# u's row moved to ScalarE's DMA queue, and its product moved behind the turning of the first k, in an RWKV and channel-mixing kernel

## The chip, the core and the metric

The kernel runs on one core of a Trainium2 chip. The metric is device microseconds of one execution: the median over several runs, and beside it one execution taken with the hardware profiler, from which all rows below come. TensorE does the matrix products, VectorE, ScalarE and GpSimd the element-wise work, and SyncE and ScalarE issue the transfers from HBM, each on a queue of its own.

## What is computed

The inputs r, k and v have shape (4, 8, 768, 48): batch, heads, steps, width of a head. Each head carries a 48x48 state that decays by w and takes in k times v; u weighs the present step's own pair. The result, laid out as (4, 768, 384), goes through a low-rank mixing over the steps (U, V) and a two-layer MLP.

```python
for t in range(S):
    cur = np.einsum('bhd,bhe->bhde', u[None] * kt, vt)
    y[:, :, t] = np.einsum('bhd,bhde->bhe', rt, state + cur)
    state = w[None, :, :, None] * state + np.einsum('bhd,bhe->bhde', kt, vt)
...
xt = x.transpose(0, 2, 1)
h = xt @ U @ V
u = x + h.transpose(0, 2, 1)
ch = np.maximum(u @ w_ch1, 0.0) @ w_ch2
return (u + ch)
```

## The kernel before

Each batch's 768 steps are cut into six chunks of 128. For a chunk n the recurrence becomes products of matrices:

- r and k are turned (transposed on TensorE against an identity, four products each, `a_tr`, L831; tiles ptr and ptk) and scaled with powers of w (rT and kT; L840 to L854).
- The score products of rT and kT (L1017) write two banks, bank_tr and bank_sc. VectorE masks them into am (L1025). TensorE multiplies am by v into pav (L1066), adds what the state of the chunks before gives (SW by rT, L1072), and collects the next state in psu (L1039).
- ks is k times a table of powers (L782). dv is the step's own term: r times k, times ub (both on GpSimd, L791), summed over a head on VectorE (dg, L798), times v (L804 on VectorE, L802 on ScalarE). VectorE adds pav and dv into x (L1085).

ub holds u on all 128 partitions. `load_ub` (L471 to L476) makes it: a DMA of 1x384 values into urow, one product p_u of a column of ones by urow, which copies the row to all partitions, and a copy to ub on ScalarE.

After the six chunks of the first batch comes what the prediction calls the G stage: x times U is gathered (c_gx, L1185, into the bank wake; gf and Gs, L1198 to L1220), V is split into parts (v_parts, L666; pv, V), x is turned (pu), and the columns uTh and uTl (high and low halves, L1268 and L1269) go into the MLP. Its first layer is p<-uTh,w1s and p<-uTl,w1s; hh and hl (L1479, L1480) are the high and low half of its result, and w2s holds the second layer's weights. The weights are unpacked and split on VectorE, ScalarE and GpSimd (L608 to L655). The MLP of one batch overlaps the recurrence of the next and runs from about 40 us to the end.

No instruction stands in its final place in the code. Every step is an operation with a key, an estimated duration, the buffers that it reads and writes, and one or more engines that can do it. `Plan.schedule` (L180 ff.) walks through time with its own estimates and picks on each engine the ready operation of the smallest key; an added `dk` shifts one operation's key. Each engine then works through its list strictly in that order. `follow` adds a semaphore wait: an element-wise operation on GpSimd waits for a VectorE operation planned just ahead, since the two engines share a port. TensorE's gaps in the plan are filled with dummy products (`wake<-still`), whose results nobody reads.

The steps that the change touches get their keys here:

```python
at(-101, lambda: ends.append(pe(214, fill, [wk], [])))
...
at(-100, lambda: load_pairs(w, wq))
at(-99, lambda: a_load(0))
...
at(UB, load_ub)
```

`a_load(n)` issues the three loads of chunk n; k of the first three chunks goes through ScalarE's queue, r and v through SyncE's. The keys of turning chunk 0's k and r are 5.0 and 5.2.

Of the kernel before, what the change touches and what calls it, by code (L numbers as in the profile page):

```python
# [47 lines left out]
class Plan:  # L48
# [36 lines left out]
    def op(self, eng, ns, fn, w=(), r=(), alt=(), lock=False, dma=0.0, rows=0, late=0.0, tiled=False, dk=0.0):  # L85


        if self.direct:
            fn()
            return None  # L90
        o = Op()
        o.n = len(self.ops)
        o.key = (self.key + dk, o.n)
        o.ways = [(eng, ns, fn, lock)] + list(alt)
        o.dma, o.rows, o.late, o.tiled = dma, rows, late, tiled
        o.deps, o.behind, o.allocs, o.bufs = set(), set(), [], []
        for acc, write in [(a, False) for a in r] + [(a, True) for a in w]:
            b, sub = acc if isinstance(acc, tuple) else (acc, None)
            if not b.uses and b.tag:
                o.allocs.append(b)  # L100
                ring = self.rings.setdefault(b.tag, {"order": [], "next": 0, "free": [(-99.0, "")] * b.bufs, "last": None})
                ring["order"].append(b)
            elif b.tag and b.uses[0][0] is not o:
                o.behind.add(b.uses[0][0])
            for p, s, pw in b.uses:
                if (write or pw) and (s is None or sub is None or s == sub) and p is not o:
                    o.deps.add(p)
            b.uses.append((o, sub, write))
            if b not in o.bufs:
                o.bufs.append(b)  # L110
                b.left += 1
        self.ops.append(o)
        return o
# [207 lines left out]
def rwkv_moe(ctx: ExitStack, tc: tile.TileContext, r, k, v, w, u, U, V, w1, w2, out):  # L321
# [9 lines left out]
    DM = H * D  # L331
# [28 lines left out]
    def wbuf(shape, dt, tag, bufs, name):  # L360
        return Buf(work, shape, dt, tag, bufs, name)
# [6 lines left out]
    def bank(tag, name):  # L368
        made = Buf(ps, [128, 512], F32, tag, {"mm": 2, "acc": 3}.get(tag, 1), name)
        if tag in ("tr", "sc"):  # L370
            if tag not in lasting:
                lasting[tag] = ps.tile([128, 512], F32, name=f"bank_{tag}", tag=tag, bufs=1)
            made.got = lasting[tag]
        return made

    def f32(ap):
        return ap.bitcast(F32)
# [4 lines left out]
    def whole(*args, **kw):  # L382

        opened.clear()
        return nc.tensor.matmul(*args, **kw)  # L385

    def pe(ns, fn, w_, r_, tiled=False, dk=0.0):
        return op("PE", ns, fn, w_, r_, tiled=tiled, dk=dk)

    def on_dve(n, fn, w_, r_, port=False, dk=0.0):  # L390
        return op("DVE", dve(n), lambda: fn(nc.vector), w_, r_, lock=port, dk=dk)

    def on_act(n, fn, w_, r_, times=1, dk=0.0):
        return op("ACT", times * (act(n) - 94) + 94, fn, w_, r_, dk=dk)
# [10 lines left out]
    def dma(fn, w_, r_, rows, run, eng="SP", ns=470, dk=0.0, late=0.0, either=False):  # L405

        q = nc.scalar if eng == "ACT" else nc.sync
        return op(eng, ns, lambda: fn(q), w_, r_, dma=rows * max(1.05, run / 320),
                  rows=rows, late=late, dk=dk, alt=[("ACT", ns, lambda: fn(nc.scalar), False)] if either else ())
# [5 lines left out]
    one_ = const.tile([1, 1], F32, name="one")  # L415
# [54 lines left out]

    def load_ub():  # L471
        urow = wbuf([1, DM], F32, "xh", NXS, "urow")
        dma(lambda q: q.dma_start(urow.t, u.rearrange("(o h) d -> o (h d)", o=1)), [urow], [], 1, 1536, ns=500)
        pt = bank("av", "p_u")
        pe(650, lambda: whole(pt.t[:, :DM], lhsT=one_.broadcast_to([1, 128]), rhs=urow.t, start=True, stop=True), [pt], [urow])
        on_act(384, lambda: nc.scalar.copy(ub.t, pt.t[:, :DM]), [ub], [pt])  # L476

    def table(i):
# [1182 lines left out]
    def at(t, f):  # L1661
        steps.append((t, len(steps), f))
# [5 lines left out]
    NEXT_W1, SOON = (18, 20), 16.0  # L1668
    MORE = {}
    FRONT, EACH = 9.0, 4.5  # L1670
    UB = -98.5
    VR, DVK, DV = 35.97, 1, -1.0
    LATE_DG = 4
    PWI, KD = 0.0, False
# [13 lines left out]
    for i, n_ in ((0, 2), (5, 1)):  # L1688
        at(-50, lambda i=i, n_=n_: on_dve(128 * n_, lambda e: e.memset(f32(sel.t[:, :, i:i + n_]), 0.0), [(sel, i)], []))
    at(UB, load_ub)  # L1690
    backs = []
    at(-97, lambda: backs.append(powers()))
# [144 lines left out]
```

## Time and profile before

| | us |
|---|---|
| median of 3 runs | 398.85 (398.24 to 399.52) |
| profiled execution | 398.65 |
| its span, first to last instruction | 396.9 |
| TensorE busy | 388.8 (98%) |
| VectorE, ScalarE, GpSimd busy | 302.3, 140.5, 97.9 |
| mean granted TensorE clock | 0.996 |

The span is the profiled execution without what lies before the first and after the last instruction (1.75 us). Busy time counts instructions of the engine itself, and a product's end is modelled, so 98% says that TensorE has nearly always an instruction in flight, not that it runs at its peak.

### The profile page before, as it was taken

The numbers are of one execution on the slowest core, as the hardware profiler recorded it, in microseconds if no ns is written. First come the engines' busy times: TensorE is split into PE (matmuls) and PEld (weight loads), VectorE is DVE, ScalarE is ACT, GpSimd is POOL, SyncE is SP. The second block draws the span as 40 slices with busy tenths as digits, with TensorE's granted clock in tenths as the row PEclk, the third lists the DMA queues.
The fourth block names the chain that finished last, engine by engine and source line by source line (L and its number), as shares of the span: only waits on it lengthen the run. The fifth ranks groups of instructions, "written<-read, shape, count | busy, mean of one in ns | idle before, by whom it ended". The sixth has DMA issues, their size and how long they took to land.

```text
span 396.9 us, 11718 instructions
## 1 busy us (share of the span) xinstructions
PE 388.8 (98%) x4808; PEld 374.3 (94%) x4808; DVE 302.3 (76%) x685; ACT 140.5 (35%) x355; POOL 97.9 (25%) x150
## 2 busy tenths in 40 slices
PE   7999999999999999999999999999999999999994
PEld 6897999999999999999999999999999999999994
DVE  6999999999999849887794588999444874455453
ACT  3378757646541422101012242541132422232210
POOL 2882142532434024331010132354000200100000
PEclk9999999999999999999999999999999999999998
DMA  9988899698759686864797768600136110000003
GB/s 147 180 212 220 166 225 255 101 201 219 132 93 208 103 192 104 150 96 86 126 157 112 142 166 130 119 2 3 61 58 143 40 61 0 2 1 2 0 3 124
DMA packets 189852, 45.08 MB, mean 114 GB/s; under 512 B 174686, under 2 KB 188256, under 8 KB 189792
## 3 DMA queue, kind: packets, MB, share of 16 engines
q1 hardware_dynamic: 186240, 43.08, 55.9%
q10 hardware_dynamic: 3552, 1.18, 1.3%
q8 instruction: 40, 0.66, 0.7%
q14 instruction: 20, 0.16, 0.2%
HBM read 36.57 MB, written 7.67 MB: 111 GB/s over the span
## 4 chain that ended last, share of the span: by engine, by line
PE 96%; DMA 1%; SPq 0%; ACT 0%; DVE 0%; issue 0%
PE p L385 65%; PE c L385 9%; PE pav L914 3%; PE pav L920 3%; PE bank_sc L385 2%; PE bank_tr L385 2%; PE bank_tr L1017 2%; DMA urow<-in_u_dram 1%; PE pav L1066 1%; PE bank_tr L894 1%; PE bank_tr L880 1%; PE bank_tr L1185 1%; PE pav L1072 1%; PE ptr L831 1%; PE pu L385 1%; PE psu L1039 1%
## 5 line engine op out<-in xcount | busy, mean ns | idle before, releaser
L385 PE MATMUL p<-uTh,w1s 128*128 128x384 f32 x432 | 111.5, 338 | 0.0
L385 PE MATMUL p<-w2s,hh 128*128 128x384 f32 x528 | 111.2, 339 | 0.0
L385 PEld LDWEIGHTS p<-w2s,hh 128*128 128x128 f32 x528 | 92.2, 188 | 1.4 <-ACT hh L1479 0.2
L1479 ACT ACTIVATE hh<-p 128x384 fp32r<-128x384 f32 x72 | 35.4, 491 | 136.2 <-PE p L385 123.9
L385 PEld LDWEIGHTS p<-uTh,w1s 128*128 128x128 f32 x432 | 77.1, 188 | 0.6
L385 PE MATMUL p<-uTl,w1s 128*128 128x384 f32 x216 | 72.4, 335 | 0.0
L385 PE MATMUL p<-w2s,hl 128*128 128x384 f32 x264 | 62.4, 335 | 0.0
L1480 DVE SCALAR_TENSOR_TENSOR hl<-p,hh 128x384 fp32r<-128x384 f32 x72 | 39.8, 553 | 28.9 <-ACT hh L1479 28.0
L385 PEld LDWEIGHTS p<-w2s,hl 128*128 128x128 f32 x264 | 47.2, 188 | 0.2 <-DVE hl L1480 0.2
L385 PEld LDWEIGHTS p<-uTl,w1s 128*128 128x128 f32 x216 | 40.5, 188 | 0.0
L781 POOL MEMSET ks<- 128x128 f32 x24 | 4.8, 206 | 70.9 <-PE bank_tr L894 70.9
L914 PEld LDWEIGHTS pav<-vsw,am 64*64 64x64 f32 x288 | 17.4, 134 | 4.5 <-issue 3.3
L1406 ACT ACTIVATE hh<-v 128x384 fp32r<-128x384 f32 x18 | 9.3, 526 | 34.8 <-DVE v L1397 31.9
L914 PE MATMUL pav<-vsw,am 64*64 64x48 f32 x288 | 19.8, 221 | 0.0
L1397 DVE TENSOR_TENSOR v<-c,s 128x384 f32<-128x384 f32 x18 | 9.9, 555 | 12.6 <-PE c L385 12.5
L914 PE MATMUL pav<-ldv,am 64*64 64x48 f32 x288 | 19.3, 221 | 0.0
L920 PE MATMUL pav<-S,rT 48*64 48x48 f32 x528 | 19.1, 218 | 0.0
L1317 POOL TENSOR_TENSOR uTl<-ut,uTh 128x384 fp32r<-128x384 f32 x4 | 4.1, 1015 | 59.1 <-ACT uTh L1316 59.1
L385 PE MATMUL c<-uTh,w1s 128*128 128x384 f32 x72 | 18.5, 338 | 0.0
L920 PEld LDWEIGHTS pav<-S,rT 48*64 48x64 f32 x528 | 17.3, 135 | 0.0
L791 POOL TENSOR_TENSOR dv<-dv,ub 128x384 f32<-128x384 f32 x12 | 12.1, 1012 | 20.3 <-DVE w2s L655 8.9
L914 PEld LDWEIGHTS pav<-ldv,am 64*64 64x64 f32 x288 | 16.9, 134 | 0.0
(253 smaller groups left out, 782.8 us busy)
## 6 DMA issues: line engine op xcount, KB each, us to landing
raw_w<-in_moe_w_ch_dram SPq DMA_DIRECT2D x24, 384.0 KB, 4.9
out_dram<-x SPq DMA_DIRECT2D x21, 192.0 KB, 2.7
ldr<-in_r_dram SPq DMA_DIRECT2D x20, 192.0 KB, 3.8
ldk<-in_k_dram SPq DMA_DIRECT2D x20, 192.0 KB, 4.2
ldv<-in_v_dram SPq DMA_DIRECT2D x20, 192.0 KB, 4.2
bl<-in_r_dram SPq DMA_DIRECT2D x79, 48.0 KB, 2.9
bl<-in_k_dram SPq DMA_DIRECT2D x79, 48.0 KB, 2.5
ub<-ud SPq DMA_DIRECT2D x15, 192.0 KB, 2.8
```

The costliest lines, as they stand in the source:

```text
L385: return nc.tensor.matmul(*args, **kw)
L781: op("POOL", 250, lambda: nc.gpsimd.memset(ks.t[:, :, D:], 0.0), [(ks, "pad")], [])
L791: on_either(384, lambda e, a_=a_, b_=b_: e.tensor_mul(dv.t, a_()[:, :, :D], b_()[:, :, :D]), w_, r_, only="POOL" if front(n) else None)
L831: nc.tensor.transpose(pt.t[:PD, q * C:(q + 1) * C], src().rearrange("p h d -> p (h d)")[:, q * PE_:q * PE_ + PD], ident_)
L914: return nc.tensor.matmul(to(q, j, i), lhsT=am[j].t[half, q, :], rhs=vsw[n].t[half, q, :] if j else vt()[half, 2 * q, :], start=((alone or ...
L920: return nc.tensor.matmul(to(q, row, i), lhsT=rT.t[rows, q, i * C2:(i + 1) * C2], rhs=St[n, i].t[rows, q, :], start=False, stop=((alone or ...
L1017: return nc.tensor.matmul(abs_[n][j].t[:, q * C:(q + 1) * C], lhsT=kT.t[rows, q, :], rhs=rT.t[rows, q, :], start=True, stop=True)
L1317: on_either(384, lambda e: e.tensor_tensor(ul.t[:, ct, :], ut.t, f32(uh.t[:, ct, :]), ALU.subtract), [(ul, ct)], [ut, (uh, ct)])
L1397: on_dve(384, lambda e: e.tensor_tensor(to.t, pt.t[:, :TB], other.t, ALU.add), [to], [pt, other])
L1406: on_act(384, lambda: nc.scalar.activation(hh.t, value(), AF.Relu), [hh], [src])
L1479: on_act(384, lambda: nc.scalar.activation(hh.t, pt.t[:, :TB], AF.Relu), [hh], [pt])
L1480: on_dve(384, lambda e: e.scalar_tensor_tensor(hl.t, pt.t[:, :TB], 0.0, f32(hh.t), ALU.max, ALU.subtract), [hl], [pt, hh])
```

## The change

urow's DMA is issued by ScalarE instead of SyncE. p_u gets a key of its own: -98.9 + 104 = 5.1, between the turning of chunk 0's k (5.0) and of its r (5.2), where it was -98.5. `UB` itself moves from -98.5 to -98.9, so the load comes right behind the loads of chunk 0 either way.

```diff
     def load_ub():
         urow = wbuf([1, DM], F32, "xh", NXS, "urow")
-        dma(lambda q: q.dma_start(urow.t, u.rearrange("(o h) d -> o (h d)", o=1)), [urow], [], 1, 1536, ns=500)
+        dma(lambda q: q.dma_start(urow.t, u.rearrange("(o h) d -> o (h d)", o=1)), [urow], [], 1, 1536, ns=500, eng="ACT")
         pt = bank("av", "p_u")
-        pe(650, lambda: whole(pt.t[:, :DM], lhsT=one_.broadcast_to([1, 128]), rhs=urow.t, start=True, stop=True), [pt], [urow])
+        pe(650, lambda: whole(pt.t[:, :DM], lhsT=one_.broadcast_to([1, 128]), rhs=urow.t, start=True, stop=True), [pt], [urow], dk=104.0)
...
-    UB = -98.5
+    UB = -98.9
```

Since the plan is made anew, other instructions move too. TensorE's list at the start, in which ld_97 and ld_116 are the loads of chunks 0 and 1, was:

```order
3 L831 MATMUL ptk_132<-ident,ld_97 112x128 x4
4 L385 MATMUL wake<-still 128x128 x2
5 L831 MATMUL ptr_148<-ident,ld_97 112x128 x4
6 L500 MATMUL pt_tabf<-ident,back 128x112 x4
7 L385 MATMUL wake<-still 128x128 x3
8 L385 MATMUL p_u<-urow,one 128x384
9 L1017 MATMUL bank_tr<-rT_170,kT_155 128x128
...
17 L831 MATMUL ptr_200<-ident,ld_116 112x128 x4
18 L831 MATMUL ptk_208<-ident,ks_113 112x128 x4
```

And it is now the following, where ld_121 is the load of chunk 1:

```order
3 L831 MATMUL ptk_133<-ident,ld_97 112x128 x4
4 L385 MATMUL p_u<-urow,one 128x384
5 L831 MATMUL ptr_149<-ident,ld_97 112x128 x4
6 L500 MATMUL pt_tabf<-ident,back 128x112 x4
7 L385 MATMUL wake<-still 128x128 x3
8 L831 MATMUL ptr_182<-ident,ld_121 112x128 x2
9 L1017 MATMUL bank_tr<-rT_173,kT_156 128x128
...
17 L831 MATMUL ptr_182<-ident,ld_121 112x128 x2
18 L831 MATMUL ptk_204<-ident,ks_111 112x128 x4
```

p_u stands in the place of the two dummy products ahead of the first r, and two of the four products that turn chunk 1's r have moved from behind the eight score products to the place ahead of them.

GpSimd's list for chunks 1 to 3, with the semaphores that each instruction waits for, was (dv_227 and dv_304 are the dv tiles of chunks 1 and 2, ks_256 the ks of chunk 2):

```order
26 L782 TENSOR_TENSOR ks_256<-ld_122,tabf 128x8x48 [waits DMAHW4_49]
27 L791 TENSOR_TENSOR dv_227<-dv_227,ub 128x384 [waits DVE_49,Pool_49]
28 L791 TENSOR_TENSOR dv_304<-ld_122 128x384 [waits DMAHW1_49]
29 L735 MEMSET ldr_317 128x8x16
30 L781 MEMSET ks_325 128x8x16 [waits PE_49]
31 L782 TENSOR_TENSOR ks_325<-ld_184,tabf 128x8x48 [waits DMAHW4_49]
```

The same place now, with chunk 1's dv called dv_236 and chunk 2's dv_306:

```order
26 L782 TENSOR_TENSOR ks_268<-ld_126,tabf 128x8x48 [waits DMAHW6_49,DVE_49,Activation_49]
27 L791 TENSOR_TENSOR dv_236<-dv_236,ub 128x384 [waits Pool_49]
28 L791 TENSOR_TENSOR dv_306<-ld_126 128x384 [waits DMAHW1_49]
29 L735 MEMSET ldr_319 128x8x16
30 L781 MEMSET ks_333 128x8x16 [waits PE_49]
31 L782 TENSOR_TENSOR ks_333<-ld_195,tabf 128x8x48 [waits DMAHW4_49,DVE_49]
```

The second dv product of chunk 1 no longer waits for VectorE; the ks products do instead.

VectorE's list at the G stage was (x_768 is the x of chunk 5):

```order
72 L1085 TENSOR_TENSOR x_768<-pav_0_707,dv_594 128x4x48
73 L1085 TENSOR_TENSOR x_768<-pav_1_733,dv_594 128x4x48
74 L655 TENSOR_TENSOR w1s_765<-raw_w_0_469,w1s_765 128x384
75 L655 TENSOR_TENSOR w1s_770<-raw_w_1_489,w1s_770 128x384
76 L615 SCALAR_TENSOR_TENSOR raw_w_0_472<-raw_w_0_472 128x384
77 L615 SCALAR_TENSOR_TENSOR raw_w_2_625<-raw_w_2_625 128x384
78 L1220 TENSOR_TENSOR Gs_787<-wake,Gs_787 32x384
```

It is now, with chunk 5's x called x_760:

```order
73 L1085 TENSOR_TENSOR x_760<-pav_0_708,dv_583 128x4x48
74 L1085 TENSOR_TENSOR x_760<-pav_1_720,dv_583 128x4x48
75 L615 SCALAR_TENSOR_TENSOR raw_w_0_477<-raw_w_0_477 128x384
76 L608 TENSOR_SCALAR raw_w_2_633<-raw_w_2_633 128x384
77 L618 SCALAR_TENSOR_TENSOR raw_w_0_477<-raw_w_0_477 128x384
78 L655 TENSOR_TENSOR w1s_777<-raw_w_0_470,w1s_777 128x384
79 L655 TENSOR_TENSOR w1s_783<-raw_w_1_488,w1s_783 128x384
80 L655 TENSOR_TENSOR w2s_788<-raw_w_0_477,w2s_788 128x384
81 L1220 TENSOR_TENSOR Gs_796<-wake,Gs_796 32x384
```

Six instructions instead of four stand between the last x and Gs. On TensorE, the pv products of that stage, which stood between the two halves of chunk 5's pav and behind gf, now stand ahead of both.

## Rows read from the trace of the kernel before

**Rows 1.** The page: busy time by engine, and the chain by line.
```profile
PE 388.8 (98%) x4808; PEld 374.3 (94%) x4808; DVE 302.3 (76%) x685; ACT 140.5 (35%) x355; POOL 97.9 (25%) x150
...
PE p L385 65%; PE c L385 9%; PE pav L914 3%; PE pav L920 3%; PE bank_sc L385 2%; PE bank_tr L385 2%; PE bank_tr L1017 2%; DMA urow<-in_u_dram 1%; PE pav L1066 1%; PE bank_tr L894 1%; PE bank_tr L880 1%; PE bank_tr L1185 1%; PE pav L1072 1%; PE ptr L831 1%; PE pu L385 1%; PE psu L1039 1%
```

**Rows 2.** The chain in order of time, 0 to 13: start us, us, what.
```profile
2.82 5.75 DMA urow<-in_u_dram
...
8.62 0.91 PE p_u L385 x2
```

**Rows 3.** Timeline of PE: start us, us, instruction [idle before <-releaser].
```profile
4.06 1.02 PE L831 MATMUL ptk<-ident,ld 128*112 128x128 f32 x4
...
6.62 0.66 PE L831 MATMUL ptr<-ident,ld 128*112 128x128 f32 x4 [1.09 <-DMA ld<-in_r_dram]
...
7.49 0.85 PE L385 MATMUL wake<-still 128*128 128x128 f32 x6
...
9.46 0.37 PE L1017 MATMUL bank_tr<-rT,kT 48*128 48x128 f32 x1
...
10.55 0.65 PE L831 MATMUL ptr<-ident,ld 128*112 128x128 f32 x4
11.03 0.60 PE L831 MATMUL ptk<-ident,ks 128*112 128x128 f32 x4
...
16.26 0.43 PE L831 MATMUL ptr<-ident,ld 128*112 128x128 f32 x2
16.62 0.67 PE L1066 MATMUL pav<-ld,am 128*64 128x48 f32 x16
```

**Rows 4.** Timeline of SyncE's queue: DMA issues.
```profile
2.82 0.92 SPq L473 DMA_DIRECT2D urow<-in_u_dram  x1
3.79 0.53 SPq L731 DMA_DIRECT2D ld<-in_r_dram  x1
```

**Rows 5.** Timeline of DVE.
```profile
7.55 1.12 DVE L844 SCALAR_TENSOR_TENSOR rT<-ptr,wif,pw 112x128 f32<-112x128 f32 x4
...
10.65 0.69 DVE L1025 TENSOR_TENSOR am<-bank_tr,before 128x512 f32<-128x512 f32 x1 [1.05 <-PE bank_sc L1017]
...
13.18 1.22 DVE L804 TENSOR_TENSOR dv<-ld,dg 128x384 f32<-128x384 f32 x1
14.32 0.68 DVE L1025 TENSOR_TENSOR am<-bank_tr,before 128x512 f32<-128x512 f32 x1
...
27.14 0.55 DVE L804 TENSOR_TENSOR dv<-ldv,dg 128x384 f32<-128x384 f32 x1
```

**Rows 6.** DMA issues in 3.5 to 4.2 us: KB each, us from issue to landing.
```profile
ld<-in_r_dram SPq DMA_DIRECT2D x1, 192.0 KB, 6.3
```

**Rows 7.** Windows: each engine's busy us, then granted clock, DMA share, GB/s.
```profile
8.00:9.00 1.00, 0.72 (x5) 0.44 (x4) 1.00 (x4) 0.17 (x1) 0.00 (x0) 1.00 1.47 164
...
391.00:392.00 1.00, 0.66 (x4) 0.34 (x2) 0.30 (x1) 0.00 (x0) 0.00 (x0) 1.00 0.46 169
...
393.00:394.00 1.00, 0.00 (x0) 0.00 (x0) 0.00 (x0) 0.00 (x0) 0.00 (x0) 0.99 0.88 309
```

**Rows 8.** Timeline of POOL.
```profile
12.99 0.99 POOL L782 TENSOR_TENSOR ks<-ld,tabf 128x384 f32<-128x384 f32 x1
14.54 1.01 POOL L791 TENSOR_TENSOR dv<-dv,ub 128x384 f32<-128x384 f32 x1 [0.56 <-DVE dv L804]
```

**Rows 9.** Timeline at the G stage: PE and DVE.
```profile
33.59 0.52 PE L385 MATMUL pv<-v_parts,sel 128*96 128x192 f32 x4 [0.50 <-ACT gf L1198]
...
40.14 0.51 PE L385 MATMUL p<-uTh,w1s 128*128 128x384 f32 x2
...
37.96 0.55 DVE L1220 TENSOR_TENSOR Gs<-wake,Gs 32x384 fp32r<-32x384 f32 x1
```

**Rows 10.** Timeline in the MLP: DVE's hl and PE's use of it.
```profile
85.85 0.56 DVE L1480 SCALAR_TENSOR_TENSOR hl<-p,hh 128x384 fp32r<-128x384 f32 x1
...
89.00 0.68 PE L385 MATMUL p<-w2s,hl 128*128 128x384 f32 x3
```

## The prediction

> **What bounds the kernel now.** I read the page first, then the chain, then the timeline of the first 45 us engine by engine, and the windows last. TensorE is busy for 388.8 of 396.9 us, and 96% of the chain is its own work; the only other piece of size is the transfer of u's row, 1% [rows 1]. The chain shows where: 5.75 us from the issue of that row, then the product p_u, 0.91 us, then chunk 0's score products [rows 2]. So the time is TensorE's work plus what it waits or fills with dummy products at the start, and something gained or lost there reaches the end only if it survives the stages between. The timeline of TensorE shows the gaps: 1.09 us before it can turn the first r, three dummy products from 7.49 to 8.34 (x6: each counts twice in the trace), p_u, and the scores at 9.46 [rows 3]. What the change takes away is the wait for urow, and p_u's place between the dummies and the scores.
>
> **The change, part by part.** *The row and its product.* urow goes out on ScalarE's queue right behind the first k, so at about 1.3 us instead of 2.82, with one 192 KB transfer ahead of it in that queue; on SyncE's it had two [rows 4]. TensorE turned that k at 4.06, so it had landed by then [rows 3], and I estimate the row at 4 to 5 us. p_u then runs behind the turning of k, in the stretch before 6.62 in which TensorE has two dummy products and waits 1.09 us [rows 3], and its 0.91 us are covered. If they are not (a row later than 5.7), they push the turn of r, and VectorE's four rT pieces at 7.55 follow that turn by 0.3 us at the earliest; the cost is then at most 0.9. With p_u gone from 8.6, the scores wait only for the rT pieces, which end at 8.67 [rows 5], and could start at about 8.7 instead of 9.46: a gain of up to 0.75 us. That is what the edit offers.
>
> *What stands in its way.* The kernel's planner lays out everything anew, and the order shows half of the second r's turning (two of four products) now ahead of chunk 0's scores. TensorE works in order, so the scores now wait for the second r to land. Before, that r was issued at 3.79 [rows 4] and took 6.3 us [rows 6]: it landed at 10.09. Without urow in SyncE's queue its issue moves up by 0.97 (3.79 less 2.82). Does the landing move too? The DMA engines were saturated when it travelled (a share of 1.47 and 164 GB/s between 8 and 9 us [rows 7]), the queue ahead of it holds the same two transfers, and the second and third k, which now go out behind urow, take bandwidth late instead of early. So it can gain nothing (10.09) or the whole 0.97 (9.12); I take 10.09, since bytes and not the issue are what it waited for.
>
> The Trainium skill's page "Trainium Kernel Development and Optimization", section "Key Constraints", says that transfers from all queues run on the same 16 DMA engines and interleave, and that issuing from several engines saves the sequencer's issue time alone. By that rule the landing stays near 10.09 and the scores are late; by the queue alone it would be 9.12. Row 8:9 of the windows agrees with the rule.
>
> *Front, summed.* Half a turn takes 0.36 us of TensorE (16.26 to 16.62, the half that before had split off in chunk 1 [rows 3]), so the scores start at 10.09 + 0.36 = 10.45, 0.99 later than 9.46. Behind the scores only the other half is left of a whole turn's 0.48 (10.55 to 11.03), so 0.24 comes back. TensorE is +0.75 at the second k's turning.
>
> *The shared port.* VectorE hangs on the scores: its mask products, 10.65 before [rows 5], start at 11.64; rT, dg and S follow, and its product dv (L804), 13.18 before, is ready at 14.17. GpSimd does not wait for it any more: before, its second dv product of chunk 1 stood at 14.54 because it waited 0.56 us for L804 [rows 8]; the order now shows it waiting for GpSimd's own work alone. It follows ks (12.99 before, whose memset waits for TensorE's psu, +0.1 to +0.2) and starts at about 14.05. What two such instructions do to each other shows in L804 itself: 1.22 us beside GpSimd's product of 12.99 to 13.98, 0.55 alone at 27.14 [rows 5, 8]. So L804 now waits from 14.17 to 15.06 and ends at 15.6; both x (0.27 each, as half as wide) and the mask product follow, at 16.1 instead of 14.32 (the order now puts both x ahead of it). Part of this +1.8 is eaten: both x stood between the two mask products before, so the second of these is only +1.2; the half turn that stood between pav and pav is gone (0.36); and the scores of chunk 2 start some +0.75 late. The whole turn behind them costs 0.24 more than the half of before. I carry +0.95 through chunks 2 to 5, which run at TensorE's own pace.
>
> *The G stage.* Chunk 5's part changes order as well. The pv products waited 0.50 us for ScalarE's gf [rows 9]; now they stand ahead of pav and wait for v_parts alone: +0.95 - 0.50 = +0.45 when the last x is made. But gf and ScalarE's Gs now come behind four casts, and VectorE's Gs, 37.96 before, behind six instructions instead of four since the last x, the two more at 0.35 to 0.55 each (L804's 0.55 alone is one of that width [rows 5]): +0.45 + 0.9 = +1.35 at Gs [rows 9], of which dummy products and turnings that are independent of it take up some 0.35 behind it. The first MLP product, 40.14 before [rows 9], comes at about +1.0. All six pu products are then done, of which two stood behind the first MLP units before; at 0.17 each (the pitch of a 384-column product) that gives 0.34 back: **+0.65**. With the r at 9.5 or earlier the same sum keeps +0.35, since the G stage costs about that by itself.
>
> *The MLP.* From there on the chain is TensorE's own [rows 1], and the order has the same 2858 instructions on it, so a shift at the entrance passes through to the end. VectorE takes 1.3 to 3.6 us more work ahead of the low halves hl (the count of added rows times their durations), and an hl stands ready some 2.6 us before its use (85.85 + 0.56 to 89.00 [rows 10]); other gaps are up to 7. I price this at nothing; its bound is the surplus over the smallest gap, 1 us, twice over in a long stage.
>
> **Rivals.** *Lost port (slower).* A waiting VectorE might lose the port a second time: GpSimd has the next product, dv of chunk 2, standing right behind, at 15.0. Then L804 starts at 16.0, and each of chunks 1 to 3 that repeats it adds about 1 us: +3.2, some 402. Nothing in the trace of before shows VectorE waiting across two back-to-back GpSimd products, so arbitration is open; it decides if L804 takes over 2 us.
> The Trainium skill's page "SBUF — State Buffer", section "Who interferes with whom", says that the order of issue decides who blocks and that the other blocks fully. By it L804 loses once, as in the sum; 1.22 against 0.55 agrees.
> *MLP stalls (slower).* The added VectorE work does overrun the slack, or TensorE's 1.75 us of nothing before 10.09 (dummies end at 8.34) takes its clock down: +1.3 to +2.3, 400.0 to 401.6. Against the clock: it was busy for 0.66 of the microsecond from 391 and then no more, and the granted clock was still 0.99 from 393 to 394 [rows 7], after over a microsecond without work; before, the longest gap at the start was 1.09 [rows 3]. Against the stalls: 2.6 us of slack.
> *The gain arrives (faster).* The second r lands at 9.1 or before, L804 misses the contention because everything comes earlier, and the G stage keeps its 0.50: -0.7 to -1.5, 397.2 to 398.0. For it: a one-transfer shorter queue and p_u's 0.75. Against it: saturated engines, and Gs behind more work.
>
> **How the numbers follow.** The sum stands against the profiled execution of 398.65, 0.20 below the median of three runs: 399.3 by the one and 399.5 by the median, so 399.4. A change under 0.3%, 1.2 us, is about what a measurement of this kernel cannot tell from none. Chances: the sum or anything within 1.2 of before, 0.55; lost port 0.10 and MLP stalls or clock 0.17, together 0.27 slower; the gain 0.18. The range leaves out the far end of the lost port and of the gain: 397.5 to 401.2.
>
> **What would show it.** Right: urow landed before 5.5 and p_u before the turn of r; TensorE idle before the half turn with the second r as releaser, 1.5 us or more; scores at 10.4; L804 of chunk 0 at about 1.4 us from when it was ready; no pv wait for gf; first MLP product at 40.8 to 41.3. Wrong: scores before 9.5, L804 at 0.55, waits of PE behind hl after 40 us, or a granted clock under 1 before 30 us.

## The result, and the profile of the changed kernel

The change makes the kernel slower by 0.5%: a median of 401.37 us over 22 runs against 399.12 us over 22 runs of the kernel before, a ratio of 1.0052 (95% interval 1.0034 to 1.0070). One execution of the changed kernel, at 428 us, was disturbed and is left out of the ratio and of the counts below. The profiled execution of the changed kernel took 400.71 us with a span of 398.9 us, 2.0 more than the span of before; of this, 1.78 us stand at the last matrix product (393.11 against 391.33) and the rest in the last transfers behind it.

The page and the chain first. TensorE is busy for 2.6 us longer than in [rows 1], and the transfer of u's row is gone from the chain; in its place the chain has 1% of VectorE. TensorE's list is no longer than before (x4805 in the page against x4808), so it is busier because it waits less (1.9 us in all up to 45 us, against 2.9) and because some products ran slower: p_u alone takes 1.64 us where it took 0.91 [rows 2]. The last section comes back to this.

```profile
PE 391.4 (98%) x4805; PEld 375.3 (94%) x4805; DVE 303.1 (76%) x691; ACT 142.7 (36%) x372; POOL 91.2 (23%) x144
...
PE 94%; DVE 1%; POOL 0%; ACT 0%; issue 0%; ACTq 0%
```

The timeline of TensorE at the start answers to [rows 3]:

```profile
4.04 1.10 PE L831 MATMUL ptk<-ident,ld 128*112 128x128 f32 x4
5.08 1.64 PE L385 MATMUL p_u<-urow,one 1*128 1x384 f32 x2
6.65 1.10 PE L831 MATMUL ptr<-ident,ld 128*112 128x128 f32 x4
...
8.29 1.51 PE L385 MATMUL wake<-still 128*128 128x128 f32 x6
10.19 0.41 PE L831 MATMUL ptr<-ident,ld 128*112 128x128 f32 x2 [0.39 <-DVE ks L782]
10.53 0.37 PE L1017 MATMUL bank_tr<-rT,kT 48*128 48x128 f32 x1
...
15.99 0.65 PE L831 MATMUL ptk<-ident,ks 128*112 128x128 f32 x4 [0.30 <-POOL ks L782]
```

p_u runs behind the turning of k without a wait, and r is turned right behind it, at 6.65 against 6.62. Then comes the half turn of chunk 1's r, at 10.19, and the scores of chunk 0 start 1.07 us later than before. The releaser printed there is VectorE's ks, which ended at 10.08; the r of chunk 1 landed at 10.02, so the two came almost together, and e7 below shows the r alone. The issue of that r on SyncE's queue moved from 3.79 [rows 4] to 2.82, and the transfer took 7.2 us instead of 6.3 [rows 6]:

```profile
2.82 1.48 SPq L731 DMA_DIRECT2D ld<-in_r_dram  x1
```

```profile
ld<-in_r_dram SPq DMA_DIRECT2D x1, 192.0 KB, 7.2
```

GpSimd and VectorE, which answer to [rows 8] and [rows 5]: here L804 takes 0.55 us, alone, and it is GpSimd that waits, with the ks of chunk 2 behind the L804 of chunk 0.

```profile
14.93 1.00 POOL L782 TENSOR_TENSOR ks<-ld,tabf 128x384 f32<-128x384 f32 x1 [1.44 <-ACT SW L1055]
15.89 1.00 POOL L791 TENSOR_TENSOR dv<-dv,ub 128x384 f32<-128x384 f32 x1
```

```profile
14.25 0.55 DVE L804 TENSOR_TENSOR dv<-ld,dg 128x384 f32<-128x384 f32 x1
```

The profile names ScalarE's SW as the releaser of ks; it ended at 14.77, and L804 at 14.80. That it is L804 which holds ks is shown by e7 below. TensorE then waits 0.30 us for this ks before it can turn it.

The G stage, VectorE's list from chunk 5's masks to the low halves uTl, answers to [rows 9]:

```profile
32.41 0.72 DVE L666 TENSOR_TENSOR v_parts<-raw_v,v_parts 128x192 fp32r<-128x192 f32 x1
33.05 0.68 DVE L1025 TENSOR_TENSOR am<-bank_tr,before 128x512 f32<-128x512 f32 x1
33.65 0.68 DVE L1025 TENSOR_TENSOR am<-bank_sc,before 128x512 f32<-128x512 f32 x1
...
36.13 0.61 DVE L1085 TENSOR_TENSOR x<-pav,dv 128x192 f32<-128x192 f32 x2
...
38.91 0.56 DVE L655 TENSOR_TENSOR w2s<-raw_w,w2s 128x384 fp32r<-128x384 f32 x1
39.69 0.55 DVE L1220 TENSOR_TENSOR Gs<-wake,Gs 32x384 fp32r<-32x384 f32 x1 [0.23 <-ACT Gs L1219]
40.28 1.03 DVE L615 SCALAR_TENSOR_TENSOR raw_w<-raw_w 128x384 int32<-128x384 int32 x2
41.22 0.56 DVE L618 SCALAR_TENSOR_TENSOR raw_w<-raw_w 128x384 int32<-128x384 int32 x1
41.81 1.49 DVE L1269 TENSOR_TENSOR uTl<-pu,uTh 128x384 fp32r<-128x384 f32 x3
```

From 32.41 to 39.47 VectorE has no pause at all; then it waits 0.23 us for ScalarE's Gs. Before, its list ran to 37.93, and Gs followed without a wait:

```profile
35.44 0.62 DVE L1085 TENSOR_TENSOR x<-pav,dv 128x192 f32<-128x192 f32 x2 [0.62 <-PE pav L1072]
...
36.91 1.02 DVE L615 SCALAR_TENSOR_TENSOR raw_w<-raw_w 128x384 int32<-128x384 int32 x2
```

TensorE's side of it: the wait of 0.50 us ahead of the pv products [rows 9] is gone, but the first MLP product comes at 41.71 instead of 40.14, and the one behind it waits for VectorE.

```profile
31.57 0.37 PE L1017 MATMUL bank_tr<-rT,kT 48*128 48x128 f32 x1
...
33.46 0.60 PE L385 MATMUL pv<-v_parts,sel 128*96 128x192 f32 x4
...
41.71 0.51 PE L385 MATMUL p<-uTh,w1s 128*128 128x384 f32 x2
42.42 0.44 PE L385 MATMUL p<-uTl,w1s 128*128 128x384 f32 x1 [0.20 <-DVE uTl L1269]
```

The chain of the changed kernel comes to Gs from TensorE, through its last products into the bank wake and ScalarE's Gs, and from there on runs through VectorE's instructions:

```profile
37.52 1.64 PE wake L385 x4
...
39.19 0.48 ACT Gs L1219
39.69 0.55 DVE Gs L1220
40.28 1.03 DVE raw_w L615 x2
41.31 0.47 DVE raw_w L618
41.81 0.57 DVE uTl L1269
42.42 2.72 PE p L385 x14
```

For chunk 5's scores and the first product on uTl, before had:

```profile
30.36 0.37 PE L1017 MATMUL bank_tr<-rT,kT 48*128 48x128 f32 x1
...
40.49 0.33 PE L385 MATMUL p<-uTl,w1s 128*128 128x384 f32 x1
```

So the loss grows in steps: +1.07 us at chunk 0's scores, +1.21 at chunk 5's (31.57 against 30.36), +1.73 at VectorE's Gs, +1.93 at the first product on uTl, +1.78 at the end. The MLP passes it on.

### The profile page after: what moved, and what is told of

Read it like the earlier page. It is cut to its first block, busy times and chain, and to the rows that moved or that the text cites. A ratio compares the mean times of both kernels' runs of the same rounds, so it can differ in the third digit from the quotient of the medians.

```text
span 398.9 us, 11735 instructions
## 1 busy us (share of the span) xinstructions
PE 391.4 (98%) x4805; PEld 375.3 (94%) x4805; DVE 303.1 (76%) x691; ACT 142.7 (36%) x372; POOL 91.2 (23%) x144
## 4 chain that ended last, share of the span: by engine, by line
PE 94%; DVE 1%; POOL 0%; ACT 0%; issue 0%; ACTq 0%
PE p L385 64%; PE c L385 9%; PE pav L914 3%; PE pav L920 3%; PE bank_sc L385 2%; PE bank_tr L385 2%; PE pav L1066 1%; PE bank_tr L894 1%; PE bank_tr L880 1%; PE bank_tr L1017 1%; PE bank_tr L1185 1%; PE pav L1072 1%; PE bank_sc L880 1%; PE bank_tr L831 1%; PE psu L1039 1%; PE ptk L831 1%
## 5 line engine op out<-in xcount | busy, mean ns | idle before, releaser
L1317 POOL TENSOR_TENSOR uTl<-ut,uTh 128x384 fp32r<-128x384 f32 x5 | 5.1, 1016 | 58.7 <-ACT uTh L1316 58.7
L802 ACT ACTIVATE dv<-ldv,dg 128x48 f32<-128x48 f32 x64 | 15.3, 322 | 7.9 <-DVE dg L798 7.9
```

The source lines that it names most:

```text
L802: nc.scalar.activation(dv.t[:, h], vt()[:, h], AF.Copy, scale=dg.t[:, h:h + 1])
L1317: on_either(384, lambda e: e.tensor_tensor(ul.t[:, ct, :], ut.t, f32(uh.t[:, ct, :]), ALU.subtract), [(ul, ct)], [ut, (uh, ct)])
```

## The experiments

Each kernel can compute both orders: `plan_as(False)` returns the list of the kernel before and `plan_as(True)` that of the changed one. `arrange` takes one of them and moves single operations; `self.ops[n]` is an operation by number, and the text says which. Lines of the helpers lie 25 to 35 further down in these kernels. e1 to e4, e5 to e8, e9 and e10, and e11 and e12 ran together, each group with its own runs of the kernel before, whose median went from 398.15 to 399.61 from group to group. Differences inside a group are therefore the safer ones. The ratio is the one on record; it is not the quotient of the two medians and differs from it by up to 0.25%.

| kernel | median us (runs) | before, same group | ratio, 95% interval |
|---|---|---|---|
| e1 edit alone | 398.69 (12) | 399.61 | 0.9956 [0.9919, 0.9994] |
| e2 half turn behind | 400.02 (12) | 399.61 | 1.0005 [0.9967, 1.0044] |
| e3 new front only | 400.76 (13) | 399.61 | 1.0010 [0.9975, 1.0044] |
| e4 new G stage only | 401.03 (12) | 399.61 | 1.0037 [0.9995, 1.0080] |
| e5 r ahead of v | 399.80 (12) | 399.01 | 1.0024 [0.9997, 1.0052] |
| e6 DMA alone | 399.18 (12) | 399.01 | 0.9994 [0.9966, 1.0022] |
| e7 no wait for L804 | 402.19 (6) | 399.01 | 1.0084 [1.0054, 1.0114] |
| e8 gf early | 402.49 (8) | 399.01 | 1.0066 [1.0022, 1.0110] |
| e9 V's parts later | 400.07 (10) | 398.15 | 1.0036 [1.0000, 1.0072] |
| e10 edit alone again | 398.79 (12) | 398.15 | 0.9994 [0.9954, 1.0035] |
| e11 more dummies | 399.86 (12) | 398.88 | 1.0021 [0.9995, 1.0047] |
| e12 half turn alone | 401.10 (12) | 398.88 | 1.0031 [0.9997, 1.0065] |

**The edit without the new order (e1, e10, e6).** e6 moves only the DMA: the row's issue goes behind the first k's (`ops[5]`), on ScalarE.

```diff
+        todo = self.plan_as(False)
+        row = self.place(todo, self.cases[0][0])
+        (o, start, end, _, _) = todo.pop(row)[1]
+        todo.insert(self.place(todo, self.ops[5]) + 1, (None, (o, start, end, "ACT", self.cases[0][2][1][0][2])))
```

e1 and e10 are one kernel, which also puts p_u behind the turning of k (`ops[60]`), in the place of two dummy products:

```diff
+        p_u = todo.pop(self.place(todo, self.cases[1][0]))
+        k = self.place(todo, self.ops[60])
+        todo = todo[:k + 1] + [p_u] + [x for x in todo[k + 1:] if isinstance(x[1], tuple) or x[0][0] > 6000]
```

Expected of e1:

> The order of before, with only the edit in it: urow's DMA behind the first k on ScalarE's queue, p_u behind the turning of that k (in the place of the two dummy products), nothing else moved. If the new order is what costs, the score products of chunk 0 start when rT is ready, at about 8.9 us instead of 9.46, and the MLP's entrance (the first uTl product, 40.49 before, 42.42 after) comes at 39.8 to 40.2: a time 0.3 to 0.7 us under before. If instead p_u's early place costs by itself, because TensorE then runs its first products at half speed (p_u 1.64 us instead of 0.91, the dummies 1.51 instead of 0.85), the entrance is at 40.6 or later and the time 0.2 to 1 us over before.

Expected of e6:

> The order of before with urow's DMA alone moved to ScalarE's queue; p_u stays behind the dummy products. p_u then loses its wait of 0.28 us: the scores start at about 9.2 instead of 9.46, the turning of the second r waits for its landing at about 10.1 (10.28 instead of 10.55), and the MLP's entrance moves by 0 to -0.3. Time: that of before within 0.3. If the place of p_u does nothing and the load does all, this one is as fast as the edit alone (0.9 us under before).

Expected of e10:

> The order of before with the edit alone, once more. If its gain is real, the ratio to before is again 0.993 to 0.999, no execution of it stands over 402 us, and no granted clock under 0.995; the second r's turning waits for its landing at about 10.1 again. If the first measurement was luck, the ratio is 0.998 to 1.002 and some executions stand at 402 to 403 as those of before do.

e1's profile has p_u at 4.89 and the scores of chunk 0 at 8.19, 1.27 us earlier than before. But the turning of chunk 1's r then waits for its landing, and most of the lead is gone:

```profile
10.23 0.62 PE L864 MATMUL ptr<-ident,ld 128*112 128x128 f32 x4 [0.89 <-DMA ld<-in_r_dram]
```

Chunk 1's scores are still 0.34 us early (12.75 against 13.09), and chunk 2's are late (17.99 against 17.84). Chunk 5's scores come at 30.52 (before 30.36) and the first product on uTl at 40.88 (before 40.49). That is where the rival of e1's expectation had it, but not for its reason, since p_u took 0.91 us here. In the G stage TensorE waited for the part of v_parts that GpSimd makes:

```profile
33.98 0.51 PE L413 MATMUL pv<-v_parts,sel 128*96 128x192 f32 x3 [0.47 <-POOL v_parts L699]
```

e1's gain of 0.4% did not come again in e10, whose ratio is 0.9994, and e6 stands at 0.9994 as well. What did come again is that no execution stands over 402 us: 0 of 36 of e1, e6 and e10, against 23 of 110 of the kernel before; whether the edit is what keeps them away was not tested further (e5, which has the edit too, has 2 of 12). In the median the edit by itself changes nothing that these runs resolve: what it takes from the start is returned from 10 us on, where the second r lands. The loss of the changed kernel comes with the order that was planned around the edit.

**The front and the G stage apart (e3, e4).** Both join the two orders at the gathering of x times U for chunks 0 to 3 (`ops[213]`, about 32 us). e3 has the changed front and before's order from there; in e4 `first, then = was, now`.

```diff
+        was = self.plan_as(False)
+        now = self.plan_as(True)
+        first, then = now, was
+        cut = first[self.place(first, self.ops[213])][0][0]
+        front = [x for x in first if x[0][0] < cut]
...
```

Expected of e3:

> The order of the changed kernel up to chunk 5's scores, and the order of before from the G stage on. If both parts cost and add up, this one keeps the front's +1.2 us alone: chunk 5's scores at 31.5, the first uTl product at about 41.7, the time 1.2 us over before. If the front's delay is absorbed by the G stage, the time is that of before within 0.3.

Expected of e4:

> The order of before up to chunk 5's scores, and that of the changed kernel from the G stage on. If the parts add up, this one costs what is left of 2.0 us: chunk 5's scores at 30.4, the first uTl product at 41.0 to 41.3, the time 0.5 to 0.8 us over before. If only the front matters, the time is that of before within 0.3.

Both are slower than e1 in the same group, by 2.1 and 2.3 us, which speaks for a cost in each part. It does not show it: against before, neither interval excludes no change, and e1 itself stood low in that group. Their profiles can't be read in absolute times: TensorE kept its lower speed until about 17 us in both (see the last section). The distance from chunk 5's scores to VectorE's Gs can: 7.47 us in e3 (34.89 to 42.36), with before's order, and 8.66 in e4 (34.75 to 43.41), with the new one. Over all profiles that distance is 7.60 in before and 7.11 to 7.83 in e1, e3, e5, e6, e10 and e12, which have before's order; it is 8.12 in the changed kernel and 8.11 to 8.66 in e2, e4, e7, e8, e9 and e11, which have the new one. So the new G order is the longer one in every profile, by 0.5 us between the kernel before and the changed one. From Gs to the first product on uTl the two take 2.53 and 2.73 us: three VectorE instructions instead of two. e4's 2.3 us are more than these distances add up to; what the rest of it is stays open.

**The half turn (e2, e12).** In e2 the half turn of chunk 1's r (`ops[75]`) goes back behind chunk 0's scores (`ops[72]`), in the new order. In e12 it goes ahead of them in before's order with the edit: e1 and two lines.

```diff
+        todo = self.plan_as(True)
+        half = todo.pop(self.place(todo, self.ops[75]))
+        todo.insert(self.place(todo, self.ops[72]) + 1, half)
```

```diff
+        half = todo.pop(self.place(todo, self.ops[75]))
+        todo.insert(self.place(todo, self.ops[72]), half)
```

Expected of e2:

> The order of the changed kernel, with the half turn of the second r put back behind chunk 0's scores. If the wait for that r is the front's loss, the scores start at about 9.0 us instead of 10.53 and chunk 5's scores at 30.2 to 30.6 instead of 31.57; the entrance of the MLP comes 0.8 to 1.3 us earlier than in the changed kernel (41.1 to 41.6), its time is 1 us under it. If the G stage sets the entrance whatever the front does (its weights come late by DMA), the entrance stays within 0.3 us of 42.42 and the time does not move.

Expected of e12:

> The order of before with the edit alone, as in e1_edit_alone, and one thing more: half of chunk 1's r turned ahead of chunk 0's scores, as in the changed kernel. Nothing else of the new order. Theory that this half turn is the front's loss and brings the clock falls: TensorE waits for chunk 1's r from about 8.4 to 10.0 us, the scores of chunk 0 start at 10.4, those of chunk 5 at 31.3 to 31.6, the MLP's first product on uTl some 0.5 us later than in e1_edit_alone (41.3 to 41.6), and 3 or more of 12 executions show a mean granted clock of 0.994 or less; the time lies 0.1 to 0.4% above before. Rival, that the front's order is harmless because the G stage takes it up, and that the clock falls belong to the rest of the new order: time as before within 0.1%, and no more than one execution with a lower clock.

e2 starts the scores at 9.83 and those of chunk 5 at 31.16, 0.41 us earlier than the changed kernel, yet its Gs stands at 39.68, and the first product on uTl at 42.40, as in the changed kernel. The row that stops it is V's: VectorE waits for ScalarE's part of v_parts and only then masks chunk 5.

```profile
32.77 0.36 DVE L696 TENSOR_TENSOR v_parts<-raw_v,v_parts 128x192 fp32r<-128x192 f32 x1 [0.75 <-ACT v_parts L695]
33.04 0.68 DVE L1055 TENSOR_TENSOR am<-bank_tr,before 128x512 f32<-128x512 f32 x1
```

ScalarE itself had waited 1.83 us for V's weights at 27.74. So the front's gain is lost at v_parts, which the new order puts ahead of chunk 5's masks. e2 is 1.3 us slower than e1 beside it: that is the new order without the half turn in front. Its ratio, 1.0005, is below the changed kernel's 1.0052, but the two come from different groups and its interval reaches 1.0044, so what the half turn alone is worth in the new order stays open.

e12 is 0.3% slower than before, with an interval that just takes in no change. Its front is the one expected, with TensorE idle for 1.66 us and r as the releaser:

```profile
9.92 0.40 PE L866 MATMUL ptr<-ident,ld 128*112 128x128 f32 x2 [1.66 <-DMA ld<-in_r_dram]
```

Chunk 5's scores (32.97) and the first product on uTl (42.61) came later than expected, because what followed was dearer than the wait. The windows of the same execution (columns: PE, PEld, DVE, ACT, POOL busy, granted clock, DMA share, GB/s) show TensorE granted half speed, 1.2 GHz, from about 11.4 to 14.8 us:

```profile
10.00:11.00 1.00, 1.00 (x14) 0.82 (x16) 0.00 (x0) 0.00 (x0) 0.92 (x2) 1.00 1.46 171
11.00:12.00 1.00, 1.00 (x11) 0.88 (x8) 0.56 (x1) 0.00 (x0) 1.00 (x2) 0.68 1.35 191
12.00:13.00 1.00, 1.00 (x9) 0.66 (x9) 1.00 (x3) 0.09 (x1) 0.86 (x2) 0.50 1.35 177
13.00:14.00 1.00, 1.00 (x24) 1.00 (x24) 0.85 (x3) 0.49 (x1) 0.03 (x1) 0.50 1.45 167
14.00:15.00 1.00, 1.00 (x27) 1.00 (x25) 0.77 (x2) 0.60 (x3) 1.00 (x2) 0.61 1.52 202
```

Chunk 1's scores came 4.96 us behind chunk 0's (15.21 less 10.25), against 3.42 in the changed kernel (13.95 less 10.53): 1.5 us.

**The idle stretch and the clock (e11).** e12 was made because of a count over the executions. The mean granted clock of an execution was 0.994 or less in 9 of 21 of the changed kernel, 4 of 13 of e3, 3 of 6 of e7 and 5 of 8 of e8, which all have the half turn ahead of the scores; in 3 of 82 of e1, e2, e4, e5, e6, e9 and e10, which don't; and in 7 of 110 of the kernel before. e12 gave 6 of 12. In the changed kernel the executions with such a clock have a median of 401.65 us, the others 400.42; in e12 it is 401.3 and 399.5. That price is not general: in e3 it is 400.9 and 400.3, and in e7 and e8 the executions with such a clock are not the slower ones (401.8 against 402.6, and 402.4 against 403.1). e11 fills the stretch ahead of the half turn with four dummy products more:

```diff
+        half = self.place(todo, self.ops[75])
+        wake = next(x for x in reversed(todo[:half]) if not isinstance(x[1], tuple))
+        todo[half:half] = [wake] * 4
```

Expected of e11:

> The changed kernel with seven dummy products instead of three between the turning of chunk 0's r and the half turn of chunk 1's r; each takes 0.14 us (at TensorE's higher speed), so they end at about 9.5 and TensorE stands idle for some 0.6 us instead of 1.7 ahead of the half turn, which r's landing still sets at 10.0. Theory that the idle stretch is what lets the granted clock fall in a part of the executions: executions with a mean granted clock of 0.994 or less become rare, at most 1 of 12 where the changed kernel had 9 of 21, and the median comes down by about 0.4 to 0.7 us against the changed kernel's, to some 0.4% above before; where TensorE is still at the lower speed when the dummies come, they take 0.25 each and can push the half turn by up to 1 us. Rival, that the falls have another cause (the new order behind the front, or chance): 4 or more of 12 executions keep such a clock.

1 of 12 executions had such a clock, and the ratio came down to 1.0021 from the changed kernel's 1.0052, although e11's profiled execution shows the price too: TensorE was still slow, the seven dummies ended at 11.00, and the first product on uTl came at 43.02. That the half turn ahead of the scores brings these falls is shown by e12, which differs from e1 and e10 in it alone: 6 of 12 against 0 of 24. That it is the idle stretch which does it rests on e11's 1 of 12, against 6 of 12 of e12 beside it and 9 of 21 of the changed kernel: likely, on a small count. It does not settle each fall: the mean misses short ones (e10's profile has 0.50 from 8 to 10 us and a mean of 0.995), and e8's fell at 7 us already, behind an idle stretch of 0.60 us.

**The wait for L804 (e7).** ks of chunk 2 (`ops[101]`, tuple `o, start, end, eng, fn`) is told to be later, so that no wait for L804 is added.

```diff
+        todo[k] = (todo[k][0], (o, start + 5000.0, end, eng, fn))
```

Expected:

> The changed kernel, in which GpSimd's ks of chunk 2 doesn't wait for VectorE's L804 of chunk 0 (the wait holds no data, it only orders the two at their port). If that wait costs on the path, ks starts at about 13.5 instead of 14.93 and the turning of chunk 2's k, 15.99 before, at 15.5; L804 is ready at 14.25 and now meets ks, so it takes 0.7 to 1.2 us instead of 0.55; chunk 5's scores come 0.2 to 0.5 earlier than 31.57. If the G stage sets the MLP's entrance, the first uTl product stays at 42.3 to 42.5 even so, and the time does not move; if the front sets it, it comes at 41.9 to 42.2.

ks starts at 13.15, TensorE's wait of 0.30 is gone, chunk 5's scores come at 31.39 instead of 31.57, and the entrance to the MLP does not move (Gs 39.65, first product on uTl 42.37). Chunks 2 and 3 start their scores 0.68 us earlier (18.02 and 22.27 against 18.70 and 22.95), and that lead is given back by chunk 5. So in this execution the wait costs nothing where it counts. The 1.0084 rests on 6 runs, 3 of them with a lower clock. Its front shows the second r by itself as the releaser of the half turn:

```profile
10.02 0.40 PE L862 MATMUL ptr<-ident,ld 128*112 128x128 f32 x2 [1.72 <-DMA ld<-in_r_dram]
```

**The G stage from inside (e8, e9).** e8 puts the gathering for chunk 4, gf and its product back to where before had them. e9 has e2's move and puts V's part on VectorE, the pv products and V's cast behind chunk 5's masks and pav.

```diff
+        for first, moved in ((213, (214, 215, 216, 217, 218)), (201, (219,))):
+            items = [todo.pop(self.place(todo, self.ops[n])) for n in moved]
+            k = self.place(todo, self.ops[first]) + 1
+            todo[k:k] = items
```

```diff
+        for first, moved in ((72, 75), (194, 210), (200, 211), (322, 212)):
+            item = todo.pop(self.place(todo, self.ops[moved]))
+            todo.insert(self.place(todo, self.ops[first]) + 1, item)
```

Expected of e8:

> The changed kernel, in which chunk 4's part of the gather, gf on ScalarE and the product of gf stand where before had them (ahead of chunk 5's pav, and right behind its SW products). If the path over gf holds Gs, Gs on VectorE comes about 1 us earlier, at 38.6 to 38.9 instead of 39.69, and the first uTl product at 41.4 to 41.6. If VectorE's six instructions between x and Gs hold it (their last ends at 39.47), Gs moves by 0.3 at most and the first uTl product, which waits behind three more of them, stays at 42.1 to 42.4.

Expected of e9:

> The changed kernel with the half turn behind chunk 0's scores, and with VectorE's v_parts behind chunk 5's two mask products and pv and V's cast behind chunk 5's pav. If VectorE's queue sets the MLP's entrance (v_parts stands ahead of the masks and waits for ScalarE's cast; from the first mask of chunk 5 at 33.05 on VectorE has no pause up to Gs), the first mask starts at 32.2 to 32.5, Gs at 38.9 to 39.2 instead of 39.69 and the first uTl product at 41.6 to 41.9 instead of 42.42. If the entrance is set elsewhere (gf's path, or the weights' casts on ScalarE), Gs stays at 39.5 to 39.7.

Neither brings Gs nearer to chunk 5's scores: 8.32 and 8.11 us, against 8.12. In e9 VectorE goes from the masks to Gs with a single pause of 0.22, nearly as dense as in the changed kernel with v_parts on the other side of the masks. e9's absolute times say nothing of its forecast, since TensorE was slow until about 16 us (chunk 5's scores at 33.52) and V's weights were there in time. e9 is 1.3 us above e10 beside it.

What holds Gs shows when e10 is laid beside the changed kernel, since both have x of chunk 5 at the same distance from its scores (4.59 and 4.56 us). Two paths meet at Gs. On VectorE, the instructions between x and Gs take 2.49 us in e10 (four, 35.78 to 38.27) and 3.34 in the changed kernel (six, 36.13 to 39.47). On TensorE, eight turnings of x now stand ahead of the last products into wake, and gf is there later; ScalarE's Gs ends at 39.67 and comes last, 0.2 us behind VectorE's list. In every profile of before's order VectorE's list ends last; in the changed kernel, e2, e4, e7 and e11 VectorE waits 0.22 to 0.32 us for ScalarE's Gs. e8, with gf earlier, takes away that wait and then has VectorE's six instructions up to 41.59, right ahead of Gs; there x itself came later, 5.06 us behind the scores. So shortening one path alone could gain some 0.2 to 0.3 us, and no run shortens both.

**The second r ahead of the first v (e5).** e1, with chunk 0's v issued behind chunk 1's r on SyncE's queue.

```diff
+        v0 = todo.pop(self.place(todo, self.ops[7]))
+        todo.insert(self.place(todo, self.ops[29]) + 1, v0)
```

Expected:

> The order of before with the edit alone, and chunk 1's r issued ahead of chunk 0's v on SyncE's queue. If the second r's landing (10.1 us whatever was taken out of the queue ahead of it) is what eats the edit's gain, it now lands 1.4 to 2 us earlier, its turning follows the scores at about 9.3 without a wait, chunk 1's scores come at 11.8 to 12.2 instead of 12.75, chunk 5's at 29.6 to 30.2, and the time is 0.4 to 0.9 us under the edit alone. If VectorE and GpSimd hold chunks 1 and 2 (their dv and ks products start at 9.67 in any order), chunk 5's scores stay at 30.3 to 30.6 and the time is that of the edit alone within 0.3.

TensorE no longer waited for that r. No gain came of it: 1.0024, with chunk 5's scores at 31.38 in a profiled execution in which TensorE was slow until 10 us. What the earlier r is worth in an execution without that was not seen.

## Why the prediction was right and wrong

Measured against the runs shown before, the ratio gives 1.0052 x 398.85 = 400.9 us: 1.5 us above the 399.4 that was named and inside its range by 0.3 us; the median of the later runs themselves, 401.37, is just outside. The direction was that of the sum, and the size was not: +0.5% instead of +0.14%, so that the likeliest case, no change that a measurement can tell, was wrong, and one of the slower cases came.

- *The row and its product*: right. The row was there at 5.08, p_u was covered, and the turn of r moved by 0.03 us. The edit's own worth was nothing that the runs resolve (e6, e10).
- *What stands in its way*: right, with its number. I took 10.09 for the second r's landing, and it was 10.02, though its issue moved up by 0.97 us. The rule of the Trainium skill's page "Trainium Kernel Development and Optimization", section "Key Constraints", that queues share the 16 engines, agrees: 6.3 us became 7.2. The scores were expected at 10.45 and came at 10.53; +0.75 at the second k's turning was +0.86 (11.89 against 11.03 [rows 3]).
- *The shared port*: the size was near, +0.95 against +1.21 at chunk 5's scores, but by luck; the mechanism failed. L804 was not blocked: it ran at 14.25 in 0.55 us, which I had named as a sign of being wrong. The order lists a wait for VectorE at GpSimd's ks, and my sum took no account of it: it was one for this very L804. The loss there was TensorE's 0.30 us, and in e7's profile that loss does not reach the MLP. What I feared did occur in e7, which lacks that wait: one L804 took 1.09 us from 21.74, beside GpSimd's dv product from 21.41 to 22.41. The Trainium skill's page "SBUF — State Buffer", section "Who interferes with whom", says that the one issued first blocks the other fully, and this row agrees roughly: L804 ended 0.42 us behind GpSimd's product, where 0.55 would be a full block.
- *The G stage*: the step that failed in size. I summed +0.65 for what the entrance to the MLP loses in all; the first second-layer product moved by +1.72 (44.14 to 45.86). I had Gs at +1.35 and it was +1.73. The two more instructions of VectorE were priced rightly (0.85 against my 0.9), and so were the 0.50 gained ahead of x (0.52); what was missing is 0.24 that came with the later scores (x at +0.69 instead of +0.45), and 0.19 for the wait for ScalarE's Gs, which I saw behind four casts and priced at nothing. Behind Gs I gave 0.35 back and 0.16 came, since VectorE had a third instruction ahead of uTl. And the 0.34 for the two pu products came back, but was lost again: TensorE's first product on uTl stood 0.71 us behind the first on uTh instead of 0.35, and small gaps took 0.14, so that this stretch cost 0.15 instead of giving 0.34.
- *What that wait was*: I booked the end of the 0.50 us wait for gf as a gain. The row names gf, but the pv products do not wait for it: in e10, whose order there is before's, they start while gf is running.

```profile
33.38 0.96 ACT L1231 COPY gf<-wake 32x96 f32<-32x96 f32 x4 [0.48 <-PE wake L1218]
```

```profile
33.85 0.60 PE L413 MATMUL pv<-v_parts,sel 128*96 128x192 f32 x4
```

What they read are the two parts of v_parts, from ScalarE and GpSimd, and the profiles of e1 and e6 name GpSimd's as the releaser, after 0.47 us. In before that part ended at 32.84 by its row, 0.75 us ahead of pv, so what ended the wait there stays open. Whatever it was, the wait was slack: with a later front before's order does not have it and takes 7.1 us from chunk 5's scores to Gs instead of 7.6 (e5, e10, e12; e3, the latest of all, 7.47), so it eats up to 0.5 us of a delay. The new order has none to give, and e2's and e7's earlier fronts gain nothing either.
- *The MLP*: right. TensorE waits nowhere behind 45 us, and the order's delay goes through.
- *The rivals*: the lost port did not happen. "The clock falls" did, in 9 of 21 executions, +1.2 us between the medians, and I held it to be part of 0.17. My argument against it was the 0.99 of one stretch at the end of the kernel [rows 7]; it did not carry over to the start.

Together: executions of the changed kernel without a lower clock stand at 400.42, 1.3 us over before's median, and I put that down to the new order (e2 against e1 and e9 against e10 give 1.3 as well, though both lack the half turn in front); with the others the median is +2.25. That the new order and not the edit costs the time is shown by the kernels with before's order: the changed kernel's interval begins at 1.0034, where e1's ends at 0.9994 and e6's at 1.0022 (e10's reaches 1.0035). How the loss divides between the half turn, the G stage and the clock is argued from single profiles. No kernel here beats the one before beyond its interval in a way that came twice.

## What to carry to other kernels

Where a planner lays out an edit anew, price the order that it makes: here the edit was worth nothing either way, and an in-order engine that got one instruction with a late input ahead of ready work lost 1 us, and sometimes its clock as well. A wait that a change removes may have been slack that absorbed delays upstream, and the releaser that a row names may only have been running at the time; before booking it as a gain, look what the instruction reads, and which paths meet at the next common point and how far apart they end. And an issue 0.97 us earlier moved the landing of r by 0.07 us while the DMA engines were loaded.

## What the runs showed of the hardware

TensorE's speed at the start differs from execution to execution, and the granted clock printed for these stretches does not show it. A stretch of six dummies (x12 in the trace) takes 2.93 us from 1.00 in every profile. Three of them later take 0.85 us when the engine is fast and 1.51 when it is not, and the change from one to the other came at about 4 us in e8 and e10, 5 in before and e1, 10 in the changed kernel, e2, e5 and e11, 16 in e9, and 17 in e3 and e4. e4's front is before's order, and this is its timeline beside [rows 3]:

```profile
4.97 1.06 PE L413 MATMUL wake<-still 128*128 128x128 f32 x4
...
9.56 1.65 PE L413 MATMUL p_u<-urow,one 1*128 1x384 f32 x2
11.13 0.58 PE L1050 MATMUL bank_tr<-rT,kT 48*128 48x128 f32 x1
```

The windows of e4 print a granted clock of 1.00 from 5 to 6 and from 9 to 10 us, where p_u took 1.65 us instead of 0.91:

```profile
5.00:6.00 1.00, 1.00 (x5) 0.74 (x4) 0.89 (x4) 0.00 (x0) 0.00 (x0) 1.00 1.48 184
9.00:10.00 1.00, 1.00 (x4) 0.78 (x4) 0.90 (x2) 0.00 (x0) 0.01 (x1) 1.00 1.43 201
```

In this execution chunk 5's scores came at 34.75 instead of 30.36 from the same order: 4.4 us of difference that belongs to no instruction of the kernel. What sets the moment of the rise was not found. A single profile's absolute times at the start must be read against it, and that is why the counts and the distances above carry the argument.
